# Loads of 48 rows for 40, separate tiles for the first two chunks' products, and later triangular inverses on GpSimd

## The chip, the cores and the metric

The kernel runs on one core of one Trainium2 chip. The metric is the device time of one execution in microseconds. The kernel before takes 633.68 us (median of three runs, 632.99 to 636.66). The core has TensorE (PE, with its weight loads shown as PEld), VectorE (DVE), ScalarE (ACT), GpSimd (POOL) and SyncE (SP). Each engine executes its own list of instructions in order and waits on semaphores for the others. All transfers of this kernel are issued from SP.

## The reference

Inputs are r, k, v, w, a, b with batch 4, heads 8, sequence 768 and head size 40: 32 independent recurrences, each with a state of 40x40. The attention output goes through a layer norm and a two-layer network (320 to 1280 to 320, in the code "moe"), and is added to it.

```python
for t in range(S):
    y[:, :, t] = np.einsum('bhd,bhde->bhe', rt, state)
    Sa = np.einsum('bhde,bhe->bhd', state, at)
    state_decay = state * wt[:, :, None, :] - np.einsum('bhd,bhe->bhde', Sa, bt)
    state = state_decay + np.einsum('bhd,bhe->bhde', vt, kt)
...
xn = (x - mu) / np.sqrt(var + 1e-06) * g_ln
ch = np.maximum(xn @ w_ch1, 0.0) @ w_ch2
return (x + ch)
```

All is fp32. The network's weights and activations are each split into a high and a low part in the reduced format fp32r, and the products are made of these parts.

## The kernel before

The sequence is cut into 24 chunks of 32 steps. The 32 recurrences lie as two halves of 16, each half's 40 head elements on partitions 0 to 39 and 64 to 103 (`ROWS`), so that an instruction over both halves covers partitions 0 to 103. Two chunks make a slab.

For each chunk, `prep(c)` loads `wa` (the decays w and the vectors a) and `bk` (k and b) in two transfers of 40 rows each. VectorE makes the running products of w by two scans with a reciprocal between (L335, L337, L339). `aT` = a times the second scan (L343) and `bk` times the first (L351) are made by VectorE for the first four chunks (`EARLY = 4`) and by GpSimd for the other twenty. `aT` is copied by two DMAs into `abd`, a tile of the other layout, of which there is one; TensorE's product L361 of `bk` and `abd` gives the chunk's two 32x32 triangles for each recurrence, which VectorE masks into `gk` (L364). From `gk` they go by DMA into `d_l` (the triangles to be inverted) and `d_k` in DRAM.

`invert(s)` handles a slab: one DMA brings the slab's `d_l` into `yv`, 64 triangles on 64 partitions. There a memset (L395) and fourteen pairs of small multiply (L403) and add (L407) instructions, with 28 to 112 elements a partition, invert the 16x16 diagonal blocks, each instruction depending on the one before. A copy on ACT (L409) transposes a part, and the result goes through DRAM (`d_h`) into the tiles `hv`. All twelve inversions are on VectorE.

`merge(c)` joins the two diagonal blocks to the inverse of the full triangle on TensorE (L428, L439, with an ACT copy L430 between). `loads(c)` brings the other operands, `x2s` from `aT` and `d_k` among them, and transposes `bk` on TensorE (L464). `chain(c)` is the recurrence from chunk to chunk: products L487, L497, L514 with ACT copies L490 and L501 between, and VectorE's state update L521. `post(c)` gives the chunk's output y (L535, L550, L567, L584, then L588 on VectorE). After each second chunk, `norm` and `moe` follow for the pair: ten groups of eight products L753, an ACT (L756) and a VectorE (L758) step, and six products L737.

`weights()` turns the network's 22 weight pieces, handed over as fp64 words, into fp32 by integer operations on VectorE (L626, L627, L630). For ten pieces it takes the sign by an ACT activation (L621) and a GpSimd product (L634) rather than by the third VectorE operation L630. Then ACT and GpSimd split them (L668, L670, L644, L659).

Every step is recorded as a task with an engine, a key, an estimated length, and what it reads and writes. `Plan.order` then walks through a model of the engines and writes each engine's list: at each step the task that could start first, ties within 0.05 us by the lower key. On PE a rule prefers the network's dense products after a sparse stretch. The chip executes these lists in order; the model's lengths decide the order only. A DMA's place on SP comes from a model of a transfer pipe (`kb` over a rate, and `queue`, how far ahead of it a transfer may be issued). A task named in `after` waits for a mark such as `"first"`, here written by chunk 1's `aT` product, which the loads of chunks 2 and 3 wait for.

Of the kernel before, what the change touches and what calls it, by code (L numbers as in the profile page):

```python
# [11 lines left out]
F32 = mybir.dt.float32  # L12
# [9 lines left out]
C = 32  # L22
# [27 lines left out]
class Plan:  # L50
# [34 lines left out]
    def order(self, free):  # L85
# [31 lines left out]
        while len(out) < len(T):  # L117
# [61 lines left out]
def body(ctx, tc, ea, eb, vr, rd, vt, w1, w1x_in, w2, gl, fe, fd, out):  # L179
# [35 lines left out]
    gk, = ring(1, "gk", 512)  # L215
# [31 lines left out]
    two = lambda x, i, n=2: [(x, i, y) for y in range(n)]  # L247

# [72 lines left out]
    def prep(c):  # L321
        i, s, j, k = c % 2, c // SLAB, c % SLAB, c % BK
        kp = c - 3.4
# [3 lines left out]
        after = [("first",)] if 2 <= c < 4 else []  # L327
        kl = kp + (0.5 if 2 <= c < 4 else -1.0 if c < 2 else 0.0)
        for hf in (1, 0):
            dma(kl - 1.3, 167, after, [W[hf]], t[ROWS[hf]], ea[c, hf])  # L330
        for hf in (1, 0):
            dma(kl - 1.1, 164, after, [K[hf]], tb[ROWS[hf]], eb[c, hf])
        R = slice(0, 104)
        n = 528
        op("DVE", 1.25, kp, W + ["start0"], [("g", i)], lambda: nc.vector.tensor_tensor_scan(  # L335
            out=flat(g[R]), data0=t[R, 0:n], data1=flat(start0[R]), initial=0.0, op0=ALU.mult, op1=ALU.max))
        op("DVE", 0.24, kp, [("g", i)], ["last"], lambda: nc.vector.reciprocal(  # L337
            out=last[R, :, C:33], in_=g[R, :, C:33]))
        op("DVE", 1.25, kp, W + ["last"], [("q", i)] + ([("go",)] if c == 0 else []), lambda: nc.vector.tensor_tensor_scan(  # L339
            out=flat(q[R])[:, ::-1], data0=t[R, n:0:-1], data1=flat(last[R])[:, ::-1], initial=0.0,  # L340
            op0=ALU.mult, op1=ALU.max))
        eng, e, us = ("DVE", nc.vector, 1.0) if c < EARLY else ("POOL", nc.gpsimd, 1.8)
        op(eng, 0.7 * us, kp, W + [("q", i)], A + ([("first",)] if c == 1 else []), lambda: e.tensor_tensor(  # L343
            out=at[R, 0:512].rearrange("p (h t) -> p h t", t=C),
            in0=t[R, 529:1041].rearrange("p (h t) -> p h t", h=16), in1=q[R, :, 1:33], op=ALU.mult))
        for hf, rs in enumerate(ROWS):
            dma(kp + 0.05, 82, A, [("abd", 0, hf)], abd[rs, hf].rearrange("p h t -> p (h t)"), at[rs, 0:512])
        op("ACT", 0.25, kp, [("g", i)], [("pc", c % AT)], lambda: nc.scalar.copy(
            out=at[R, 512:528], in_=g[R, :, C:33].rearrange("p h o -> p (h o)")))
        kb = tb[R].rearrange("p (h x t) -> p h x t", h=16, x=2)  # L350
        op(eng, 1.25 * us, kp, [("g", i)], K, lambda: e.tensor_tensor(  # L351
            out=kb, in0=kb, in1=g[R, :, 0:C].unsqueeze(2).broadcast_to([104, 16, 2, C]), op=ALU.mult))
# [3 lines left out]
        def f(b=b):  # L356
            pg = bank[b.at].rearrange("p (f n t) -> p f n t", f=2, t=C)
            for h in range(8):
                for bb in range(2):
                    p = 8 * bb + h  # L360
                    mm(pg[64 * bb:64 * bb + 64, :, h], lhsT=tb[R, 64 * p:64 * p + 64], rhs=abd[R, :, p],  # L361
                       start=True, stop=True)
        op("PE", 1.08, kp + 0.3, K + two("abd", 0), [b], f, opens=[b], room=["gk"], recs=32)
        op("DVE", 0.68, kp + 0.3, [b, "sign"], ["gk"], lambda b=b: nc.vector.tensor_tensor(  # L364
            out=gk.rearrange("p (n t) -> p n t", t=C), in0=bank[b.at].rearrange("p (n t) -> p n t", t=C),
            in1=sign.unsqueeze(1).broadcast_to([128, 16, C]), op=ALU.mult))
# [13 lines left out]
        op("ACT", 0.62, c - 1.8, [("q", i)], ["qc"], lambda: nc.scalar.copy(  # L380
# [6 lines left out]
    def invert(s):  # L387

        n, c0 = 32 * SLAB, SLAB * s
        k0 = c0 - 2.0  # L390
# [4 lines left out]
        op("DVE", 0.15, k0, (), ["y"], lambda: nc.vector.memset(y[:, 0:1024:33], 1.0))  # L395
        yb = y.rearrange("p (i x) -> p i x", i=2)[:, :, 0:512].rearrange("p i (a t) -> p i a t", t=C)[:, :, :, 0:B]
        for j in range(1, B - 1):
# [3 lines left out]
            def f(j=j, m=m, S=S):  # L401
                tv = tmp[0:n, 0:2 * m * j].rearrange("p (i a t) -> p i a t", i=2, t=j)
                nc.vector.tensor_tensor(  # L403
# [3 lines left out]
                nc.vector.tensor_tensor(out=v, in0=v, in1=tv, op=ALU.add)  # L407
            op("DVE", 0.6, k0 + 0.02 * j, (), ["y", "ytmp"], f)
# [35 lines left out]
    def loads(c):  # L444
        i = c % 2
        at = aT[c % AT]
        for hf, rs in enumerate(ROWS):
            vs = slice(VROW[hf], VROW[hf] + C)
            dma(c - 1.2, 84, [("aT", c % AT), ("pc", c % AT)], [("x2s", i, hf)], x2s[i][rs, hf], at[rs])
# [3 lines left out]
            dma(c - 0.6, 82, (), [("r", i, hf)], x5s[i][rs, hf], rd[c, hf])  # L453
            dma(c - 0.6, 82, (), [("vT", i, hf)], vu[i][rs, :, 0], vr[c, hf])

        tb = bk[c % BK]
        for bb in range(2):
# [8 lines left out]
            op("PE", 0.4, c - 1.2 + 0.1 * bb, two("bk", c % BK) + ["ident"], bs, f, opens=bs, room=X, recs=16)  # L466
# [11 lines left out]
    def chain(c):  # L478
        i, o = c % 2, (c + 1) % 2
        b = Bank("A")  # L480
# [8 lines left out]
        op("PE", 0.75, c, two("x2s", i, 4) + two("S", i, 4) + two("v", i), [b], f, opens=[b], room=[("hn", i)], recs=64)  # L489
        op("ACT", 0.46, c, [b], [("hn", i)], lambda b=b: nc.scalar.mul(  # L490
# [7 lines left out]
        op("PE", 0.72, c, [("tt", i), ("hn", i)], [b], f, opens=[b], room=[("u", i)], recs=64)  # L498
        for q, qs in enumerate(QUADS):
            hf, bb = q % 2, q // 2  # L500
            op("ACT", 0.44, c, [b], [("u", i)], lambda b=b, qs=qs, hf=hf, bb=bb: nc.scalar.copy(  # L501
                out=x2[i][UROW[hf]:UROW[hf] + C, hf, 8 * bb:8 * bb + 8],
                in_=bank[b.at][qs, 0:CH].rearrange("p (h e) -> p h e", e=D)))
        if c + 1 < NCH:
            for bb in range(2):
# [10 lines left out]
                op("PE", 0.75, c, two("xk1", i, 4) + [("eye", i), ("u", i)] + two("S", i, 4) + two("v", i), [b], f, opens=[b],  # L516
# [438 lines left out]
```

## Time and profile before

| | before |
|---|---|
| time, median of 3 runs | 633.68 us |
| profiled execution | 636.37 us |
| its span | 634.6 us |
| mean granted TensorE clock | 0.942 of full speed |
| first triangle product L361 starts | 14.67 us |
| first inversion (L395) starts | 36.93 us |
| first merge L428 starts | 52.07 us |
| busy VectorE / GpSimd | 446.5 / 117.6 us |

All times of the profile count from the start of the span. The profiled execution is 0.4% above the median, and 1.8 us of it lie around the span. A row of a group reads: line, engine, operation, output and inputs with shapes, count; then busy time and mean time of one; then idle time of the engine just before, with what ended most of it. A timeline row has the start and the length ahead and the same idle time in brackets. In the windows, each row is a stretch of the span with its length, each engine's busy time and count of instructions, the granted clock, the DMA engines' share and GB/s.

### The profile page before, as it was taken

What the parts mean: (1) busy time and instruction counts of PE and PEld (TensorE: products, weight loads), DVE (VectorE), ACT (ScalarE), POOL (GpSimd) and SP (SyncE); (2) the same over time, 40 slices, a digit from 0 to 9 for tenths busy, and PEclk for the clock granted to TensorE, in tenths of its full rate; (3) what the DMA queues carried; (4) which work ended last, traced back from release to release, by engine and by line L of the source; (5) the groups of instructions that cost most, each with busy time, mean ns of one, the idle gap of its engine ahead of it and who ended that gap; (6) DMA issues with size and microseconds to landing.
All of it is one profiled execution on the core that took longest, in us unless ns stands there. A gap on an engine that the chain in (4) does not pass through costs nothing.

```text
span 634.6 us, 35137 instructions
## 1 busy us (share of the span) xinstructions
PE 537.4 (85%) x15610; PEld 489.7 (77%) x15610; DVE 446.5 (70%) x1114; ACT 323.6 (51%) x836; POOL 117.6 (19%) x109
## 2 busy tenths in 40 slices
PE   0714875888959989899989999999789899999995
PEld 0514764777858879889989988888779799888995
DVE  7588699996488695595785885864876845967742
ACT  9726756664434454564455355354256545644421
POOL 9108055612021220120221021021022100000000
PEclk9999975798969999999989999799799999999998
DMA  6666667365654554446556356446445445452200
GB/s 170 160 176 171 158 161 206 78 155 121 158 152 125 139 134 106 127 122 156 141 127 163 92 138 151 102 112 159 108 122 143 113 106 119 117 134 79 88 32 25
DMA packets 132205, 81.63 MB, mean 129 GB/s; under 512 B 102736, under 2 KB 108880, under 8 KB 132048
## 3 DMA queue, kind: packets, MB, share of 16 engines
q1 hardware_dynamic: 132048, 79.32, 48.8%
q8 instruction: 124, 2.03, 1.3%
q14 instruction: 33, 0.27, 0.2%
HBM read 51.64 MB, written 12.58 MB: 101 GB/s over the span
## 4 chain that ended last, share of the span: by engine, by line
PE 57%; DVE 16%; issue 8%; SPq 6%; DMA 6%; ACT 4%; POOL 2%; DVEq 0%; ACTq 0%; POOLq 0%
PE bank L737 15%; PE bank L753 13%; SPq L253 6%; PE bank L514 4%; PE bank L567 4%; DVE ytmp L403 3%; DVE yv L407 3%; PE bank L361 3%; PE bank L550 3%; PE bank L584 2%; PE bank L464 2%; PE bank L487 2%; PE bank L439 2%; PE bank L535 2%; PE bank L497 2%
## 5 line engine op out<-in xcount | busy, mean ns | idle before, releaser
L737 PE MATMUL bank<-w,hh 128*128 128x320 f32 x480 | 120.2, 336 | 0.0
L753 PE MATMUL bank<-xh,w 128*128 128x256 f32 x480 | 109.2, 289 | 2.2 <-DVE hl L758 1.7
L756 ACT ACTIVATE hh<-bank 128x256 fp32r<-128x256 f32 x120 | 46.1, 384 | 125.3 <-PE bank L753 123.1
L758 DVE SCALAR_TENSOR_TENSOR hl<-bank,hh 128x256 fp32r<-128x256 f32 x120 | 50.3, 420 | 68.3 <-ACT hh L756 65.6
L753 PEld LDWEIGHTS bank<-xh,w 128*128 128x128 f32 x480 | 83.8, 192 | 3.4 <-DVE hl L758 2.0
L351 POOL TENSOR_TENSOR bk<-bk,gE 104x1024 f32<-104x1024 f32 x20 | 45.9, 2294 | 217.5 <-DMA bk<-in_eb_dram 140.3
L737 PEld LDWEIGHTS bank<-w,hh 128*128 128x128 f32 x480 | 79.7, 196 | 3.8
L737 PE MATMUL bank<-w,hl 128*128 128x320 f32 x240 | 76.1, 317 | 0.1
L753 PE MATMUL bank<-xl,w 128*128 128x256 f32 x240 | 68.4, 285 | 1.2 <-DVE xl L725 1.2
L361 PE MATMUL bank<-abd,bk 104*64 104x64 f32 x768 | 32.1, 245 | 35.8 <-POOL mask L266 14.7
L403 DVE TENSOR_TENSOR ytmp<-yv 64x28 f32<-64x28 f32 (+6 forms) x168 | 43.2, 257 | 23.3 <-issue 11.1
L469 ACT COPY xk<-bank 64x320 f32<-64x320 f32 x96 | 40.2, 418 | 35.3 <-PE bank L464 30.9
L361 PEld LDWEIGHTS bank<-abd,bk 104*64 104x64 f32 x768 | 28.8, 157 | 38.0 <-POOL mask L266 14.6
L521 DVE TENSOR_TENSOR x<-bank,x2s 40x320 f32<-40x320 f32 x92 | 44.6, 485 | 10.6 <-PE bank L514 8.4
L514 PE MATMUL bank<-x,xk 128*40 128x40 f32 (+1 forms) x1472 | 43.1, 220 | 9.2 <-ACT x L501 6.1
L514 PEld LDWEIGHTS bank<-x,xk 128*40 128x40 f32 (+1 forms) x1472 | 36.8, 133 | 15.4 <-ACT x L501 6.8
L553 ACT COPY xk<-bank 40x320 f32<-40x320 f32 x96 | 40.2, 418 | 15.2 <-PE bank L550 13.8
L407 DVE TENSOR_TENSOR yv<-yv,ytmp 64x28 f32<-64x28 f32 (+6 forms) x168 | 43.5, 259 | 5.8
L737 PEld LDWEIGHTS bank<-w,hl 128*128 128x128 f32 x240 | 46.9, 195 | 0.7 <-DVE hl L758 0.6
L753 PEld LDWEIGHTS bank<-xl,w 128*128 128x128 f32 x240 | 46.2, 193 | 1.5 <-DVE xl L725 1.5
L573 DVE TENSOR_TENSOR x5s<-bank,mask 64x256 f32<-64x256 f32 x96 | 40.5, 422 | 9.0 <-PE bank L567 6.7
L335 DVE TENSOR_TENSOR_SCAN gE<-wa,start 104x528 f32<-104x528 f32 x24 | 30.8, 1283 | 20.8 <-DMA wa<-in_ea_dram 11.8
(122 smaller groups left out, 1046.5 us busy)
## 6 DMA issues: line engine op xcount, KB each, us to landing
wa<-in_ea_dram SPq DMA_DIRECT2D x48, 162.7 KB
bk<-in_eb_dram SPq DMA_DIRECT2D x48, 160.0 KB
xk<-xk SPq DMA_DIRECT2D x48, 160.0 KB
x2s<-aT SPq DMA_DIRECT2D x48, 82.5 KB
wa<-in_ea_dram SPq DMA_DIRECT2D x24, 165.0 KB
rbd<-in_rd_dram SPq DMA_DIRECT2D x48, 80.0 KB
x<-in_vt_dram SPq DMA_DIRECT2D x48, 80.0 KB
abd<-aT SPq DMA_DIRECT2D x48, 80.0 KB
```

Source lines behind the costliest of these rows:

```text
L351: op(eng, 1.25 * us, kp, [("g", i)], K, lambda: e.tensor_tensor(out=kb, in0=kb, in1=g[R, :, 0:C].unsqueeze(2).broadcast_to([104, 16, 2, C] ...
L361: mm(pg[64 * bb:64 * bb + 64, :, h], lhsT=tb[R, 64 * p:64 * p + 64], rhs=abd[R, :, p], start=True, stop=True)
L403: nc.vector.tensor_tensor(out=tv, in0=yb[:, :, j + 1:, j:j + 1].broadcast_to(S), in1=yb[:, :, j:j + 1, 0:j].broadcast_to(S), op=ALU.mult)
L407: nc.vector.tensor_tensor(out=v, in0=v, in1=tv, op=ALU.add)
L469: op("ACT", 0.45, c - 1.2 + 0.1 * bb, [bs[hf]], [X[hf]], lambda b=bs[hf], zs=zs, hf=hf, bb=bb: nc.scalar.copy(out=xk[i][zs, 1, hf, 8 * bb: ...
L514: mm(pst[ROWS[hf], h], lhsT=xk[i][FROW[hf], 1, hf, p], rhs=x2[i][FROW[hf], hf, p], start=True, stop=True)
L521: nc.vector.tensor_tensor(out=x2[o][rs, hf, ps], in0=bank[b.at][rs, 0:CH].rearrange("p (h e) -> p h e", e=D), in1=x2s[o][rs, hf, 512 + 8 * ...
L573: op("DVE", 0.4, c + 0.5, [b, "mask"], [("z", i)], lambda b=b, zs=zs, ps=ps, hf=hf, bb=bb: nc.vector.tensor_tensor(out=x5s[i][zs, hf, 8 * ...
L737: mm(bank_of(po[u])[:, 0:CH], lhsT=l[:, us], rhs=ws[f"w2_{f}"][:, x], start=f == 0 and n == 0, stop=f == 9 and n == 2)
L753: mm(ph, lhsT=l, rhs=r, start=n == 0, stop=n == 7)
L756: yield "ACT", 0.39, [phs[f]], [("hh", f % 2)], lambda f=f: nc.scalar.activation(out=hht[f % 2], in_=bank_of(phs[f])[:, 0:256], func=AF.Re ...
L758: yield "DVE", 0.42, [phs[f], ("hh", f % 2)], [("hl", f % 2)], lambda f=f: nc.vector.scalar_tensor_tensor(out=hlt[f % 2], in0=bank_of(phs[ ...
```

## The change

- The loads of `wa` and `bk` and of `x2s` from `aT`, r, `rbd` and v's transposed form, and the copy into `abd`, take 48 rows of each half rather than 40. The host arrays are padded with eight rows; the scans and products cover 112 partitions rather than 104.
- For chunks 0 and 1 VectorE writes a times the second scan into the product's tile itself, in two instructions of 48 rows: chunk 0 into `abd`, chunk 1 into `rbd`. ACT copies it back into `aT`. Chunk 1's `gk` is the otherwise unused third `aT` tile. The mark `"first"` is now written by chunk 1's `gk` and gates chunk 2's loads; a mark `"second"`, at the end of the first inversion, gates chunk 3's.
- `EARLY` is 2: `aT` and `bk` of chunks 2 and 3 are GpSimd's.
- The keys of chunks 0 and 1 in merge, chain, post and norm are lower by 2.0 (`soon`), those of the first inversion by 4.
- Inversions of slabs 1 to 11 are on GpSimd, with the same 29 instructions each.
- All 22 weight pieces take the sign by the third VectorE operation.

```diff
+DP = 48
+LROWS = [slice(r, r + DP) for r in HROW]
-EARLY = 4
+EARLY = 2
...
-                pipe = max(pipe, end + 1.3) + t["kb"] / 200.0
+                pipe = max(pipe, end + 1.3) + t["kb"] / 240.0
...
+    soon = lambda c: 2.0 if c < SLAB else 0.0
...
-        kp = c - 3.4
+        kp = c - 3.4 - soon(c)
-        after = [("first",)] if 2 <= c < 4 else []
+        after = [("first",)] if c == 2 else [("second",)] if c == 3 else []
+        ab, an = (rbd, "rbd") if c == 1 else (abd, "abd")
+        gk, gn = (aT[2][:, 0:512], ("aT", 2)) if c == 1 else (gk1, "gk")
-            dma(kl - 1.3, 167, after, [W[hf]], t[ROWS[hf]], ea[c, hf])
+            dma(kl - 1.3, 200, after, [W[hf]], t[LROWS[hf]], ea[c, hf], queue=low)
...
+        if c < 2:
+            for hf, rs in enumerate(LROWS):
+                op("DVE", 0.7, kp, W + [("q", i)], [(an, 0, hf)], lambda hf=hf, rs=rs: nc.vector.tensor_tensor(
+                    out=ab[rs, hf], in0=t[rs, 529:1041].rearrange("p (h t) -> p h t", h=16), in1=q[rs, :, 1:33],
+                    op=ALU.mult))
+                op("ACT", 0.65, kp + 1.0, [(an, 0, hf)], A, lambda hf=hf, rs=rs: nc.scalar.copy(
+                    out=at[rs, 0:512].rearrange("p (h t) -> p h t", t=C), in_=ab[rs, hf]))
+        else:
...
-        op("DVE", 0.68, kp + 0.3, [b, "sign"], ["gk"], lambda b=b: nc.vector.tensor_tensor(
+        op("DVE", 0.68, kp + 0.3, [b, "sign"], [gn] + ([("first",)] if c == 1 else []), lambda b=b: nc.vector.tensor_tensor(
...
-        k0 = c0 - 2.0
+        eng, e, us = ("DVE", nc.vector, 0.54) if s == 0 else ("POOL", nc.gpsimd, 0.75)
+        k0 = c0 - 2.0 - 2 * soon(c0)
-        op("DVE", 0.15, k0, (), ["y"], lambda: nc.vector.memset(y[:, 0:1024:33], 1.0))
+        op(eng, 0.15, k0, (), ["y"], lambda: e.memset(y[:, 0:1024:33], 1.0))
-            op("DVE", 0.6, k0 + 0.02 * j, (), ["y", "ytmp"], f)
+            op(eng, us, k0 + 0.02 * j, (), ["y", "ytmp"] + ([("second",)] if s == 0 and j == B - 2 else []), f)
...
-                if sel:
-                    nc.scalar.activation(out=hi.bitcast(F32), in_=hi.bitcast(F32), func=AF.Sign)
-                if not sel:
-                    nc.vector.scalar_tensor_tensor(
-                        out=m, in0=hi, scalar=0x80000000, in1=m, op0=ALU.bitwise_and, op1=ALU.bitwise_or)
-            if sel:
-                op("POOL", 0.9, key, [res] + sg, [("ot", mi)], lambda: nc.gpsimd.tensor_tensor(
-                    out=m.bitcast(F32), in0=m.bitcast(F32), in1=hi.bitcast(F32), op=ALU.mult))
...
-    def rows(x):
-        return x.reshape(NCH, 2, 16, C, D).transpose(0, 1, 4, 2, 3)
+    def rows(x, pad=0):
+        y = np.full((NCH, 2, DP, 16, C), pad, np.float32)
+        y[:, :, :D] = x.reshape(NCH, 2, 16, C, D).transpose(0, 1, 4, 2, 3)
+        return y
```

New line numbers that answer to old ones: scans L343, L347 (L335, L339); the products into `abd` and `rbd` L353; `aT` L359 (L343); `bk` L367 (L351); triangle product L379 (L361); `gk` L382 (L364); inversion L415, L423, L427, L429 (L395, L403, L407, L409); merge L448 (L428); `weights` L646, L647, L649 (L626, L627, L630); weight parts L686 (L670).

VectorE's list in the opening, from chunk 1's first scan (before). `gE` and `qE` are the scans' outputs, `bank_144` and `bank_146` the products of chunks 0 and 1:

```order
L335 SCALAR_TENSOR_TENSOR gE_79<-wa_74,start_0_71 104x528
L337 RECIPROCAL last_72<-gE_79 104x16
L339 SCALAR_TENSOR_TENSOR qE_81<-wa_74,last_72 104x528
L343 TENSOR_TENSOR aT_83<-wa_74,qE_81 104x512
L351 TENSOR_TENSOR bk_76<-bk_76,gE_79 104x1024
L364 TENSOR_TENSOR gk_87<-bank_144,sign_70 128x512
L335 SCALAR_TENSOR_TENSOR gE_78<-wa_73,start_0_71 104x528
L364 TENSOR_TENSOR gk_87<-bank_146,sign_70 128x512
```

Between these and the first inversion (L395) stand the rest of chunk 2, chunk 3's scans and products, a weight piece and chunk 2's `gk`. The same place after the change:

```order
L343 SCALAR_TENSOR_TENSOR gE_79<-wa_74,start_0_71 112x528
L345 RECIPROCAL last_72<-gE_79 112x16
L382 TENSOR_TENSOR gk_87<-bank_144,sign_70 128x512
L347 SCALAR_TENSOR_TENSOR qE_81<-wa_74,last_72 112x528
L353 TENSOR_TENSOR rbd_86<-wa_74,qE_81 48x512 x2
L367 TENSOR_TENSOR bk_76<-bk_76,gE_79 112x1024
L382 TENSOR_TENSOR aT_84<-bank_147,sign_70 128x512
L343 SCALAR_TENSOR_TENSOR gE_78<-wa_73,start_0_71 112x528
L345 RECIPROCAL last_72<-gE_78 112x16
L347 SCALAR_TENSOR_TENSOR qE_80<-wa_73,last_72 112x528
L415 MEMSET yv_89 64x32
```

Chunk 0's `gk` moved ahead of chunk 1's second scan, chunk 1's `gk` ahead of chunk 2's scans, and the inversion follows right behind chunk 2's scans.

SP's list from the first `d_l` transfers to the first `yv` load, before (`d_l_176` holds the first slab's triangles; `aT_84` is chunk 2's, `bk_75` chunk 3's, this `wa_73` chunk 4's):

```order
L253 DMA d_l_176<-gk_87 32x16x32 x2
L253 DMA d_k_153<-gk_87 32x512 x2
L253 DMA abd_85<-aT_84 40x512 x2
L253 DMA bk_75<-in_eb_dram 40x1024
L253 DMA wa_73<-in_ea_dram 40x1041
L253 DMA yv_89<-d_l_176 64x1024
```

These are chunk 1's `d_l` and what follows. The same place after (`aT_84` is here chunk 1's `gk`, `wa_73` and `bk_77` are chunk 2's loads):

```order
L257 DMA d_l_176<-aT_84 32x16x32 x2
L257 DMA d_k_153<-aT_84 32x512 x2
L257 DMA wa_73<-in_ea_dram 48x1041 x2
L257 DMA bk_77<-in_eb_dram 48x1024
L257 DMA yv_89<-d_l_176 64x1024
```

The two copies into `abd` and the loads of chunks 3 and 4 are gone from between, and chunk 2's loads have moved there from ahead of `d_l`.

GpSimd's list at the later weight pieces, before (`w_8`, `w_9` are pieces of the second layer, `m` and `ot` their work tiles):

```order
L634 TENSOR_TENSOR m_143<-m_143,r_8_219 128x320
L351 TENSOR_TENSOR bk_75<-bk_75,gE_78 104x1024
L670 TENSOR_TENSOR w_8_1828<-m_143,w_8_1828 128x320
L634 TENSOR_TENSOR ot_141<-ot_141,r_9_220 128x320
L670 TENSOR_TENSOR w_9_1924<-ot_141,w_9_1924 128x320
L343 TENSOR_TENSOR aT_82<-wa_73,qE_80 104x512
L351 TENSOR_TENSOR bk_76<-bk_76,gE_79 104x1024
```

After the change, slab 2's inversion (`yv_89` and `ytmp_90`, a memset and 28 instructions) stands between the last two pieces. Its last three rows and what follows:

```order
L427 TENSOR_TENSOR yv_89<-yv_89,ytmp_90 64x2x2x13
L423 TENSOR_TENSOR ytmp_90<-yv_89 64x28
L427 TENSOR_TENSOR yv_89<-yv_89,ytmp_90 64x2x14
L686 TENSOR_TENSOR w_9_2048<-ot_141,w_9_2048 128x320
L359 TENSOR_TENSOR aT_83<-wa_74,qE_81 112x512
L367 TENSOR_TENSOR bk_76<-bk_76,gE_79 112x1024
```

The signs' products L634 are gone, and piece `w_9` and the `aT` product behind it wait in this list until the 28 instructions of the inversion are through.

More of the change, by code (lines that the diff above doesn't have):

```diff
@@ L488, in f @@
                        rhs=x2[i][RROW[hf], hf, p], start=True, stop=True)
[L489 to L490 removed]
+        op("PE", 0.75, k, two("x2s", i, 4) + two("S", i, 4) + two("v", i), [b], f, opens=[b], room=[("hn", i)], recs=64)
+        op("ACT", 0.46, k, [b], [("hn", i)], lambda b=b: nc.scalar.mul(
             out=hn[i], in_=bank[b.at][:, 0:CH].rearrange("p (h e) -> p h e", e=D), mul=-1.0))
```

137 lines of the change are left out of this document (72 added, 65 removed).

## The prediction

> **What bounds the kernel now.** The page comes first: busy shares, TensorE's row in 40 slices, then the chain that ended last, by engine.
>
> ```profile
> PE 537.4 (85%) x15610; PEld 489.7 (77%) x15610; DVE 446.5 (70%) x1114; ACT 323.6 (51%) x836; POOL 117.6 (19%) x109
> PE   0714875888959989899989999999789899999995
> q1 hardware_dynamic: 132048, 79.32, 48.8%
> PE 57%; DVE 16%; issue 8%; SPq 6%; DMA 6%; ACT 4%; POOL 2%; DVEq 0%; ACTq 0%; POOLq 0%
> ```
>
> TensorE carries most of the chain, but its holes lie in the first third; VectorE's 16% of the chain is mostly there. The windows by stage say how much (columns: length, then busy us of PE, PEld, DVE, ACT, POOL, then granted clock, DMA share, GB/s).
>
> ```profile
> 60.00:123.00 63.00, 43.61 (x1358) 37.71 (x1352) 53.99 (x119) 42.60 (x106) 30.71 (x31) 0.76 0.58 156
> 123.00:184.00 61.00, 49.96 (x1612) 44.66 (x1600) 43.11 (x119) 28.93 (x76) 8.42 (x7) 0.93 0.59 145
> 184.00:548.00 364.00, 344.00 (x10443) 314.74 (x10442) 254.08 (x678) 182.15 (x484) 51.09 (x29) 0.96 0.51 127
> 548.00:634.00 86.00, 78.18 (x1706) 73.73 (x1694) 50.55 (x121) 31.09 (x85) 0.00 (x0) 0.98 0.28 79
> ```
>
> PE is busy in the last four stages for 43.6+50.0+344.0+78.2 = 515.8 us, so for only 21.6 of the first 60. Its work hardly changes, so the gain must come out of its holes: 38 us before 60, 30.4 between 60 and 184, 20.0 up to 548, and 8 in the tail. In 60:123 VectorE is 86% busy: there it is the bound, and PE's granted clock is 0.76.
>
> **Part one: the first two chunks.** The timeline of the opening (start, duration, engine, line; in brackets idle time and its releaser):
>
> ```profile
> 7.76 1.26 DVE L339 TENSOR_TENSOR_SCAN qE<-wa,last 104x528 f32<-104x528 f32 x1
> 9.67 1.22 DVE L351 TENSOR_TENSOR bk<-bk,gE 104x1024 f32<-104x1024 f32 x1
> 10.08 2.22 SPq L253 DMA_DIRECT2D abd<-aT  x2
> 14.67 1.98 PE L361 MATMUL bank<-abd,bk 104*64 104x64 f32 x32 [14.67 <-POOL mask L266]
> 19.56 0.74 SPq L253 DMA_DIRECT2D abd<-aT  x1
> 23.18 1.97 PE L361 MATMUL bank<-abd,bk 104*64 104x64 f32 x32
> 23.48 1.26 DVE L335 TENSOR_TENSOR_SCAN gE<-wa,start 104x528 f32<-104x528 f32 x1 [6.04 <-DMA wa<-in_ea_dram]
> 25.26 0.69 DVE L364 TENSOR_TENSOR gk<-bank,sign 128x512 f32<-128x512 f32 x1 [0.52 <-PE bank L361]
> 26.61 0.86 SPq L253 DMA_DIRECT2D d_l<-gk  x2
> 32.06 0.53 SPq L253 DMA_DIRECT2D yv<-d_l  x1
> 36.93 0.09 DVE L395 MEMSET yv<- 64x32 f32 x1
> 44.42 0.64 ACT L409 COPY yv<-yv 64x256 f32<-64x256 f32 x1 [8.03 <-DVE yv L407]
> 52.07 1.56 PE L428 MATMUL bank<-hv 32*32 32x16 f32 x64 [0.50 <-DMA hv<-d_h]
> L343 DVE TENSOR_TENSOR aT<-wa,qE 104x512 f32<-104x512 f32 x4 | 2.8, 692 | 0.1
> ```
>
> The mask is named beside 14.67, but the product doesn't read it; the copy into `abd`, issued at 10.08, does end about there. Both chunks shared one `abd`, so the second copy (last half issued 19.56) stood behind the first product and d_l, d_k. Without copies, by these durations: scan ends 9.0; the 48-row halves cost what 104 rows cost if time goes by elements per row, 2 x 0.69, to 10.4; `bk` 1.22, to 11.6, when the first product can start (14.67 now, 3 earlier). Chunk 1: first scan and reciprocal to 13.2, chunk 0's gk 13.6 to 14.3, second scan to 15.6, two halves to 17.0, `bk` to 18.2, product to 20.2, gk to 20.9 (25.95 now, 5 earlier). The four copies back to aT go to ACT; its queue holds only constants there.
>
> d_l to yv's issue is 5.45 us now, with four other transfers between; with d_k, wa and one bk between I take 4, so about 25, landing 4.9 later (32.06 to 36.93) at 30. But VectorE has chunk 2's scans ahead of the inversion, and their load now waits for chunk 1's gk: issued near 23, landing near 27, scans to 30. Hence inversion at 30 (36.93 now) and first merge 15.1 later, at 45. **Term one: -7**, bounds -10 (yv alone decides) and -3 (only the first product moves). The copies, d_l and wa queue on SP, so a late gk 1 delays all behind it.
>
> Chunk 3 gets no such lead: its load waits for the end of the first inversion, so the second slab's triangles reach `yv` about when they do now. I give it zero.
>
> **Part two: VectorE relieved, GpSimd loaded.** Groups (busy us, mean ns of one):
>
> ```profile
> L407 DVE TENSOR_TENSOR yv<-yv,ytmp 64x28 f32<-64x28 f32 (+6 forms) x168 | 43.5, 259 | 5.8
> L403 DVE TENSOR_TENSOR ytmp<-yv 64x28 f32<-64x28 f32 (+6 forms) x168 | 43.2, 257 | 23.3 <-issue 11.1 <-DMA d_h<-d_l 3.7 <-DMA x2s<-aT 3.3
> L351 DVE TENSOR_TENSOR bk<-bk,gE 104x1024 f32<-104x1024 f32 x4 | 4.9, 1220 | 0.0
> L630 DVE SCALAR_TENSOR_TENSOR ot<-r,ot 128x256 uint32<-128x256 uint32 x7 | 4.1, 582 | 0.2
> L351 POOL TENSOR_TENSOR bk<-bk,gE 104x1024 f32<-104x1024 f32 x20 | 45.9, 2294 | 217.5 <-DMA bk<-in_eb_dram 140.3 <-DMA hv<-d_h 26.4 <-PE bank L720 20.1
> L343 POOL TENSOR_TENSOR aT<-wa,qE 104x512 f32<-104x512 f32 x20 | 24.6, 1231 | 106.6 <-DVE qE L339 53.5 <-DMA x2s<-aT 15.7 <-DMA x2s<-d_k 14.8
> L659 POOL TENSOR_TENSOR w1x<-ot,w1x 64x320 fp32r<-64x320 f32 x4 | 3.6, 891 | 28.7 <-issue 28.4
> L634 POOL TENSOR_TENSOR ot<-ot,r 128x320 f32<-128x320 f32 x6 | 5.3, 877 | 5.5 <-ACT qm L430 2.8 <-ACT ot L644 1.6 <-ACT w L668 1.1
> L267 POOL TENSOR_SCALAR_AFFINE_SELECT sign<-sign 32x32 f32<-32x32 f32 x4 | 0.8, 207 | 0.3
> ```
>
> VectorE loses 11/12 of 86.7 = 79.5 us, and 2 x (0.69+1.22) = 3.8; it gains 2 x 0.69 for the split products and 10 x 0.58 for the third bit operation of ten weight pieces: net -76, over the whole span. In 60:123 it is 28 x 0.258 = 7.2 less and up to 5.8 more, so VectorE stays loaded there; what goes is that the weight conversions stand behind an 11 us block. In 123:184 two blocks go, 14 us of 43. ACT sheds ten Sign activations, GpSimd ten products of 0.88.
>
> GpSimd's price for the small triangle operations isn't in the trace. Through 512 and 1024 elements a line has 2.08 ns an element and 168 ns fixed; 28 operations average 80 elements (sum of 2j(15-j) over 14 steps = 1120), so 0.33 us, and with 0.07 us of hand-over about 11.3 us an inversion: an estimate. Below: the select's 207 ns for 32 elements gives 28 x 0.28 = 7.8. Above: L659's 891 ns for 320 elements gives 27. I take the line, since both its points are two-operand products in fp32 on this engine; the upper end stays in the range.
>
> What an inversion may last is read at a steady one:
>
> ```profile
> 338.20 0.69 DVE L364 TENSOR_TENSOR gk<-bank,sign 128x512 f32<-128x512 f32 x1
> 348.86 0.09 DVE L395 MEMSET yv<- 64x32 f32 x1
> 360.43 0.67 ACT L409 COPY yv<-yv 64x256 f32<-64x256 f32 x1 [0.76 <-DVE yv L407]
> 370.43 0.72 PE L428 MATMUL bank<-hv 32*32 32x16 f32 x64
> ACT yv L409 <- DVE yv L407: 20.9, 7, 8.0
> PE bank L514 <- ACT x L501: 6.1, 3, 4.8
> ```
>
> It lasts 11.6 us on VectorE, since other work is mixed in, and 32.2 from gk to merge. GpSimd at 11.3, plus at most one chunk's `aT` and `bk` (3.5) ahead of it, is 11 to 15. I put the break-even at 16, an estimate: 11.6 and some 4 us of the waits that come back between landing and merge. Beyond it ACT's copy L409 waits, with the state's copies queued behind it, and TensorE behind those (the last row's 6.1 us).
>
> **Term two, 60 to 184: -10**, a third of the 30.4 us of holes; bounds 0 (GpSimd returns it) and -20. **Term three, 184 to 548: -6**, under a third of the 20.0; bounds -18 and, for slow inversions, the rival's price.
>
> A port conflict shows in the trace:
>
> ```profile
> 116.25 2.29 POOL L351 TENSOR_TENSOR bk<-bk,gE 104x1024 f32<-104x1024 f32 x1
> 116.51 2.37 DVE L627 SCALAR_TENSOR_TENSOR ot<-r,ot 128x320 uint32<-128x320 uint32 x1
> ```
>
> The VectorE operation ends when GpSimd's does plus its own length. With 28 short operations an inversion, VectorE waits for 0.33 us at a time rather than 2.3, but GpSimd waits a whole scan of 1.26. Two chunks' scans inside an inversion add up to 5 us to its 11.3: 16, the break-even. The Trainium skill, "SBUF — State Buffer", section "SBUF: two separate sides", says that VectorE operations with two SBUF inputs and GpSimd hold the shared port pair exclusively for a whole instruction. These two rows agree; it speaks against this change.
>
> **Part three: loads of 48 rows.** At most all bytes of the queue grow by a fifth: 48.8% becomes 58.6%, what 60:184 bears already. I take zero, bounds -3 and +3. The row for a gain:
>
> ```profile
> DVE gE L335 <- DMA wa<-in_ea_dram: 11.8, 5, 6.0
> ```
>
> The Trainium skill, "DMA: Bandwidth & Descriptors", section "Why a DMA increments its semaphore by 16 and not by 1", says that a transfer uses the largest number of engines up to 16 that divides its slowest dimension: 10 for 40 rows, 16 for 48, so 4 rows each become 3. By it the sum would be about 3 us lower (a quarter of 11.8); no row here counts engines.
>
> **The sum.** -7-10-6 = -23 from the profiled execution's 636.37 (span 634.6 and 1.8 around it): 613.4. The median, 633.68, is 0.42% below that execution, so 611.
>
> **Rivals.** (a) *GpSimd's inversions are late.* At 0.70 us an operation (nearer to L659's 0.89), an inversion is 19.6, 3.6 over the break-even; ten slabs make +36, less terms one and two, 17: 636.4+19 = 655, so 653. It decides from 16 us upward, and overtakes the gains at 16+1.7. For: the upper row, the locked port. Against: the line. The Trainium skill, "GPSIMD Engine Reference", section "Performance pitfalls for Q7 kernels", charges 50% more an element when reads step over 8 bytes, as these do; by it 13.7 us, still under 16.
> (b) *Only the opening moves.* TensorE is 94.5% busy in 184:548, and conversions and GpSimd's weight parts refill the middle: -7, so 627.
> (c) *TensorE closes its holes.* With the middle at -20 and the stage to 548 at -18: -45, so 589. For: VectorE's 76 us; against: the chain of state remains.
> (d) *Exchange without gain.* The early weight conversions, now all on VectorE, and weight parts standing behind an inversion on GpSimd eat term one: 632 to 636.
>
> **Chances.** Forecast 0.48, (a) 0.09, (b) 0.20, (c) 0.13, (d) 0.10. A change under 1% (627.3 to 640.0) can hardly be told from none. Forecast and (c) are faster, (b) straddles the bound and is put at 0.12 faster, 0.08 same; (d) is same. Faster 0.73, same 0.18, slower 0.09. The forecast's own range is 600 to 623; the range 590 to 634 takes in (b), most of (c) and (d), and leaves out (a).
>
> **What would show it.** First products at about 11.6 and 18, first merge near 45; inversion from memset to ACT's copy 11 to 15 us on GpSimd, mean operation 0.33; VectorE busy near 370; PE's holes in 60 to 184 cut by a third; PE's busy time unchanged within 1%. The forecast is wrong if the mean operation is over 0.5 us, if ACT's wait for the inversions grows beyond the 20.9 us of before, or if the holes of 60 to 184 stay near 30 us.

## The result and the profile after

The changed kernel takes 685.25 us (median of four, 681.11 to 690.38) against 634.66 us in the same comparison: 1.08 times the time before, 95% interval 1.071 to 1.089. The forecast was 611, range 590 to 634. It missed the sign. Rival (a) had the sign and 653. Here and below a time is the median of all executions of a run, while a ratio with its interval leaves out executions in a slower state that some fall into and compares with the kernel before in the same comparison, so the two need not agree to the last figure.

The page after the change, the rows that answer to those of before:

```profile
span 681.8 us, 35117 instructions
PE 555.0 (81%) x15610; PEld 506.3 (74%) x15610; DVE 374.9 (55%) x803; ACT 318.6 (47%) x830; POOL 229.6 (34%) x422
PE   1514793789689979959989989899799898799996
q1 hardware_dynamic: 142640, 86.88, 54.7%
PE 36%; POOL 14%; DMA 13%; SPq 13%; DVE 9%; issue 8%; ACT 6%; POOLq 0%; DVEq 0%; ACTq 0%
```

VectorE was relieved as forecast, to 374.9 us, and the kernel is slower all the same. TensorE's share of the chain fell from 57% to 36%. GpSimd (2% before) has 14%, transfers and their issue on SP have 26% (12% before). The span grew by 47.2 us: 17.6 are more busy time of PE with the same instructions (mean granted clock 0.912 for 0.942), 29.6 are more holes. By stage (columns as before):

```profile
60.00:123.00 63.00, 42.01 (x1346) 37.30 (x1346) 51.39 (x96) 38.89 (x100) 34.27 (x53) 0.74 0.70 170
123.00:184.00 61.00, 51.82 (x1579) 46.69 (x1574) 38.10 (x74) 27.34 (x73) 31.86 (x64) 0.87 0.74 152
184.00:548.00 364.00, 323.91 (x9520) 295.49 (x9521) 177.62 (x408) 166.49 (x446) 125.00 (x236) 0.92 0.56 131
548.00:681.00 133.00, 117.93 (x2648) 110.17 (x2646) 66.64 (x159) 49.47 (x131) 11.19 (x29) 0.95 0.32 85
```

The holes up to 184 are what they were within 2 us (70.9 for 68.8). Between 184 and 548, the stage where I had seen 6 us to gain, they doubled from 20.0 to 40.1. The steady inversion answering to the one shown of before, from the slab's second gk to its merge (timeline; the last row is the DMA into `hv`):

```profile
452.33 0.69 DVE L382 TENSOR_TENSOR gk<-bank,sign 128x512 f32<-128x512 f32 x1
466.97 0.15 POOL L415 MEMSET yv<- 64x32 f32 x1
480.26 0.63 ACT L429 COPY yv<-yv 64x256 f32<-64x256 f32 x1 [4.02 <-POOL yv L427]
482.40 0.41 ACT L523 COPY x<-bank 32x320 f32<-32x320 f32 x1
490.44 0.20 PE L448 MATMUL bank<-hv 32*32 32x16 f32 x2 [1.75 <-DMA hv<-d_h]
486.94 1.84 SPq L257 DMA_DIRECT2D hv<-d_h  x4
```

38.1 us from gk to merge for 32.2. The inversion lasts 13.3 us for 11.6, from the memset to ACT's copy. ACT stands idle for 4.0 of them with the state's copies L523 queued behind it. One slab isn't the rule: of the 5.9 us more, 4.0 lie ahead of its inversion. On the mean of the fourth to the eleventh slab, gk to memset takes 13.1 us for 12.3, and memset to last add 12.6 for 10.5. What else waits is in the view of waits (total, times, longest):

```profile
DVE gE L343 <- DMA wa<-in_ea_dram: 47.2, 10, 10.2
ACT yv L429 <- POOL yv L427: 34.5, 10, 4.8
PE bank L448 <- DMA hv<-d_h: 19.5, 10, 10.5
```

Before, VectorE waited 11.8 us for `wa`, and ACT 20.9 us for the inversions. So two candidates stand side by side: inversions that end late for ACT, and transfers that land late for VectorE and TensorE.

### The profile page after: what moved, and what is told of

It reads as the page before. It is cut to its first block, busy times and chain, and to the rows that moved or that the text cites. A ratio compares the mean times of both kernels' runs of the same rounds, so it can differ in the third digit from the quotient of the medians.

```text
span 681.8 us, 35117 instructions
## 1 busy us (share of the span) xinstructions
PE 555.0 (81%) x15610; PEld 506.3 (74%) x15610; DVE 374.9 (55%) x803; ACT 318.6 (47%) x830; POOL 229.6 (34%) x422
## 4 chain that ended last, share of the span: by engine, by line
PE 36%; POOL 14%; DMA 13%; SPq 13%; DVE 9%; issue 8%; ACT 6%; POOLq 0%; DVEq 0%; ACTq 0%
SPq L257 12%; PE bank L769 10%; PE bank L753 9%; POOL ytmp L423 6%; POOL yv L427 6%; DMA yv<-d_l 4%; PE bank L590 2%; PE bank L536 2%; DMA wa<-in_ea_dram 2%; DMA hv<-d_h 2%; PE bank L379 2%; DMA abd<-aT 1%; PE bank L607 1%; PE bank L573 1%; PE bank L448 1%
## 5 line engine op out<-in xcount | busy, mean ns | idle before, releaser
L753 PE MATMUL bank<-w,hh 128*128 128x320 f32 x480 | 123.4, 344 | 0.0
L769 PE MATMUL bank<-xh,w 128*128 128x256 f32 x480 | 114.9, 300 | 0.6 <-ACT xh L740 0.6
L367 POOL TENSOR_TENSOR bk<-bk,gE 112x1024 f32<-112x1024 f32 x22 | 51.0, 2319 | 165.1 <-DMA bk<-in_eb_dram 106.8
L769 PEld LDWEIGHTS bank<-xh,w 128*128 128x128 f32 x480 | 89.4, 205 | 1.7 <-ACT xh L740 1.0
L343 DVE TENSOR_TENSOR_SCAN gE<-wa,start 112x528 f32<-112x528 f32 x24 | 33.4, 1396 | 61.8 <-DMA wa<-in_ea_dram 47.2
L423 POOL TENSOR_TENSOR ytmp<-yv 64x28 f32<-64x28 f32 (+6 forms) x154 | 60.1, 391 | 11.2
L427 POOL TENSOR_TENSOR yv<-yv,ytmp 64x28 f32<-64x28 f32 (+6 forms) x154 | 55.6, 361 | 12.1
L490 ACT COPY xk<-bank 64x320 f32<-64x320 f32 x96 | 40.1, 418 | 34.9 <-PE bank L485 33.4
L543 DVE TENSOR_TENSOR x<-bank,x2s 40x320 f32<-40x320 f32 x92 | 44.6, 485 | 13.8 <-PE bank L536 11.6
L359 POOL TENSOR_TENSOR aT<-wa,qE 112x512 f32<-112x512 f32 x22 | 26.1, 1186 | 76.1 <-DMA x2s<-aT 41.6
L769 PEld LDWEIGHTS bank<-xl,w 128*128 128x128 f32 x240 | 49.5, 206 | 0.3 <-DVE xl L741 0.3
L379 PE MATMUL bank<-abd,bk 104*64 104x64 f32 x736 | 31.4, 247 | 20.9 <-DMA x<-in_vt_dram 12.2
L576 ACT COPY xk<-bank 40x320 f32<-40x320 f32 x96 | 40.1, 417 | 15.4 <-PE bank L573 13.9
L523 ACT COPY x<-bank 32x320 f32<-32x320 f32 x96 | 40.0, 416 | 12.9 <-PE bank L519 11.4
```

The source lines that it names most:

```text
L423: e.tensor_tensor(out=tv, in0=yb[:, :, j + 1:, j:j + 1].broadcast_to(S), in1=yb[:, :, j:j + 1, 0:j].broadcast_to(S), op=ALU.mult)
L427: e.tensor_tensor(out=v, in0=v, in1=tv, op=ALU.add)
L543: nc.vector.tensor_tensor(out=x2[o][rs, hf, ps], in0=bank[b.at][rs, 0:CH].rearrange("p (h e) -> p h e", e=D), in1=x2s[o][rs, hf, 512 + 8 * ...
L753: mm(bank_of(po[u])[:, 0:CH], lhsT=l[:, us], rhs=ws[f"w2_{f}"][:, x], start=f == 0 and n == 0, stop=f == 9 and n == 2)
L769: mm(ph, lhsT=l, rhs=r, start=n == 0, stop=n == 7)
```

## The experiments

**The inversions back on VectorE (e1), the inversions alone on GpSimd (e2).**

```diff
 e1, changed kernel:
-        eng, e, us = ("DVE", nc.vector, 0.54) if s == 0 else ("POOL", nc.gpsimd, 0.75)
+        eng, e, us = ("DVE", nc.vector, 0.54)
 e2, kernel before:
+        eng, e, us = ("DVE", nc.vector, 0.6) if s == 0 else ("POOL", nc.gpsimd, 0.75)
...
-                nc.vector.tensor_tensor(out=v, in0=v, in1=tv, op=ALU.add)
+                e.tensor_tensor(out=v, in0=v, in1=tv, op=ALU.add)
```

> The changed kernel with all twelve inversions on VectorE, nothing else undone. Theory one (GpSimd's inversions, 12.8 us from memset to last add, hold up the merges and with them the state): 625 to 640, at least 45 of the 51 us come back. Theory two (the transfers: more bytes in the loads of 48 rows and another order on SP hold up scans and merges): 665 to 685, since all transfers stay.

> The kernel before with only the inversions of slabs 1 to 11 moved to GpSimd. Theory one: 665 to 695, the whole loss with none of the other edits. Theory two: 630 to 645.

e1: 669.72 us, 1.057 [1.049, 1.065]. e2: 654.69 us, 1.029 [1.021, 1.038]. e1 lies in theory two's range, e2 between the two. Neither theory holds alone: of some 50 us, GpSimd's inversions explain 15 to 20.

**40 rows in the changed kernel (e3), and a shorter inversion in unchanged lists (e4).**

```diff
 e3:
-DP = 48
+DP = 40
-        LR = slice(0, 112)
+        LR = slice(0, 104)
 e4:
+            skip = s > 0 and j % 2 == 1 and j < B - 2
...
+                if skip:
+                    return
```

> The changed kernel with loads, scans and products of 40 and 104 rows as before; GpSimd keeps its inversions. Theory one: 675 to 690, no change. Theory two: 635 to 655.

> The changed kernel with six of the fourteen pairs left out in the inversions of slabs 1 to 11 (those of steps 1, 3, 5, 7, 9 and 11; this part of the inverse is not computed). Every engine's list is otherwise the same, row by row, so this run has no other order. An inversion lasts about 7.3 us in place of 12.8. Theory one: 11 slabs get 5.5 us each sooner, 630 to 655. Theory two, or a loss that comes from the order alone: 675 to 690.

e3: 678.68 us, 1.070 [1.062, 1.077]. e4: 666.04 us, 1.051 [1.041, 1.061]. With six of the fourteen pairs gone and every list as it was, an inversion lasts 6.6 us on average for 12.7. 11 slabs x 6.1 us gave back only 19 us, though no wait of ACT for GpSimd's inversions is left. So the length of the inversion does set part of the pace, a little under a third of a microsecond per microsecond, and something else sets the rest.

**The other parts, each alone: the gate of chunk 3 (e5), the opening (e6), 48 rows (e7), the conversions (e8).** The three on the kernel before take over the change's own lines for that part (in e8 these also enter VectorE's three operations on a piece as three tasks rather than one); of each, the line that marks it:

```diff
 e5, changed kernel:
-        after = [("first",)] if c == 2 else [("second",)] if c == 3 else []
+        after = [("first",)] if 2 <= c < 4 else []
 e6, kernel before (with the lines for chunks 0 and 1 that follow from it, and soon):
+EARLY = 2
+        after = [("first",)] if c == 2 else [("second",)] if c == 3 else []
 e7, kernel before:
+            dma(kl - 1.3, 200, after, [W[hf]], t[LROWS[hf]], ea[c, hf])
 e8, kernel before:
-                    nc.scalar.activation(out=hi.bitcast(F32), in_=hi.bitcast(F32), func=AF.Sign)
```

> The changed kernel, with chunk 3's loads again waiting only for chunk 1's triangles (mark first), not for the end of the first inversion (mark second). In the changed kernel chunk 3's gk ends at 73.7 us, before at 52.4. Theory three (this gate delays the second slab by some 20 us, and the delay is never made up): gk of chunk 3 near 52 to 56, total 650 to 668. If the delay is absorbed later, 675 to 690.

> The kernel before with the opening edits alone: two chunks' products written into their tiles, EARLY 2, the lower keys, chunk 2 waiting for first and chunk 3 for second; 40 rows, the old conversions, all inversions on VectorE, the old transfer rate. Theory three: 645 to 660, most of the 35 us that stayed with the inversions back on VectorE. My first forecast for this part was 627; if the loss lies in the rows, the conversions or the transfer rate, 622 to 636.

> The kernel before with the padded arrays and loads, scans and products of 48 and 112 rows, nothing else. By the trace of the change (scans 1.40 for 1.28 to 1.47 us, 86.9 for 79.3 MB): 636 to 645; if transfers carry the rest of the loss, 655 or more; by the rule that 48 rows use more engines, 625 to 632.

> The kernel before with the sign of all 22 weight pieces taken by VectorE's third operation, nothing else. VectorE gets 5.8 us more in its fullest stretch, ACT and GpSimd lose 5 and 10: 632 to 642. If the early VectorE load carries the rest of the loss, 650 or more.

e5: 678.27 us, 1.060 [1.049, 1.071]. e6: 643.95 us, 1.011 [1.005, 1.016]. e7: 648.54 us, 1.018 [1.010, 1.027]. e8: 630.55 us, 0.987 [0.979, 0.995].

The opening loses where I had taken 7 us. In e6, chunk 3's gk and chunk 2's output, then the same two before the change (VectorE's timeline):

```profile
73.67 0.69 DVE L382 TENSOR_TENSOR gk<-bank,sign 128x512 f32<-128x512 f32 x1
145.49 0.49 DVE L611 TENSOR_TENSOR xt<-bank,pi 128x320 f32<-128x320 f32 x1
```

```profile
51.66 0.69 DVE L364 TENSOR_TENSOR gk<-bank,sign 128x512 f32<-128x512 f32 x1 [0.67 <-DMA hv<-d_h]
123.75 0.49 DVE L588 TENSOR_TENSOR xt<-bank,pi 128x320 f32<-128x320 f32 x1 [0.67 <-PE bank L584]
```

The second slab comes 22 us late; later chunks make up most of it, and 1.1% remain. Undoing the gate alone in the changed kernel (e5) gave back 7 us by the medians and 2% by the ratios (1.060 for 1.080, intervals that just touch), less than theory three asked for. Chunk 3's gk moved only from 73.00 to 63.59 there, where theory three had 52 to 56. The 48 rows lose without any other edit; the page of e7:

```profile
q1 hardware_dynamic: 142896, 87.27, 59.4%
PE 54%; DVE 13%; DMA 12%; issue 7%; SPq 6%; ACT 5%; POOL 0%; DVEq 0%; ACTq 0%; POOLq 0%
```

10% more bytes take 24% more of the engines' time (59.4% of 645.5 us for 48.8% of 634.6), and transfers' share of the chain doubles from 6% to 12%. Only the conversions gain, and little is to spare: their interval ends at 0.995.

**The transfer assumption of the ordering (e9, e10), the gainful parts of the opening (e11), and GpSimd's price in the ordering (e12).**

```diff
 e9, changed kernel:
-                pipe = max(pipe, end + 1.3) + t["kb"] / 240.0
+                pipe = max(pipe, end + 1.3) + t["kb"] / 200.0
 e10, kernel before: 200.0 to 240.0 on the same line
 e11, from e6, with the conversions of e8:
-EARLY = 2
+EARLY = 4
+    soon = lambda c: 0.0
+        after = [("first",)] if 2 <= c < 4 else []
 e12, from e2:
-        eng, e, us = ("DVE", nc.vector, 0.6) if s == 0 else ("POOL", nc.gpsimd, 0.75)
+        eng, e, us = ("DVE", nc.vector, 0.6) if s == 0 else ("POOL", nc.gpsimd, 0.95)
```

> The changed kernel with the old assumption on transfers in the ordering (200 for 240 KB a us, so the order of all engines changes, the work doesn't). The four parts tried alone on the kernel before come to +20, +7, +12 and -8 us, +31 together, where the whole change costs 50. If the assumption carries the rest: 655 to 670. If the rest is that the parts make each other worse (an inversion on GpSimd behind later transfers): 675 to 690.

> The kernel before with the new assumption (240 for 200), nothing else. If it carries the rest: 645 to 655. If the parts make each other worse: 628 to 640.

> The kernel before with the gainful parts alone: the first two chunks' products written into their own tiles without DMA, and all signs on VectorE; 40 rows, EARLY 4, the old keys, both loads waiting for first, inversions on VectorE. If the opening's loss came from chunks 2 and 3 being held back: first merge near 45 to 48, gk of chunk 3 near 46 to 52, total 618 to 630. If direct products bring nothing to the end: 628 to 634, as with the conversions alone.

> The kernel before with the inversions of slabs 1 to 11 on GpSimd as in e2, but the ordering reckons with 0.95 us a pair, near the 0.91 measured, in place of 0.75. If e2's loss comes from lists that expect the inverse too early (ACT's copy and TensorE's merge standing in front of other work): 630 to 642. If the latency itself, or VectorE and GpSimd waiting for each other, costs it: 648 to 660.

e9: 673.02 us, 1.053 [1.046, 1.059]. e10: 641.54 us, 1.004 [1.000, 1.009]. e11: 631.64 us, 0.989 [0.983, 0.996], no better than the conversions alone. e12: 634.06 us, 0.989 [0.984, 0.995]: the same work on the same engines as e2, and e2's 20 us are gone. ACT's waits, first e2, then e12:

```profile
ACT yv L410 <- POOL yv L408: 26.3, 9, 6.8
```

```profile
ACT yv L410 <- POOL yv L408: 3.1, 1, 3.1
```

The number is only an entry in the ordering. At 0.75 a pair the lists reckon with an inversion of 10.65 us; e2's lasted 12.6 on average where its copy waited. With 0.95 the lists put more network work ahead of ACT's copy: the last slab's copy stands behind 95 of the 120 network groups in e12, and behind 86 in e2. In the kernel before, GpSimd isn't too slow; the lists expected it too early.

**Does the price explain the changed kernel (e13, e14), and does it act without GpSimd (e16)?** e14 has e3's edit, the 200 of e9 and the 0.95; e15 is e11 with e12's line.

```diff
 e13, changed kernel:
-        eng, e, us = ("DVE", nc.vector, 0.54) if s == 0 else ("POOL", nc.gpsimd, 0.75)
+        eng, e, us = ("DVE", nc.vector, 0.54) if s == 0 else ("POOL", nc.gpsimd, 0.95)
 e16, kernel before:
-            op("DVE", 0.6, k0 + 0.02 * j, (), ["y", "ytmp"], f)
+            op("DVE", 0.42, k0 + 0.02 * j, (), ["y", "ytmp"], f)
```

> The changed kernel with 0.95 for 0.75 us a pair in the ordering, nothing else; all work the same. Theory four (the lists reckon with an inversion of 10.5 us where the chip takes 12.5 to 12.8, and ACT's copy, standing too early, stops its queue): ACT's wait for GpSimd's inversions falls from 34.5 to under 10 us and the total to 650 to 665; the 48 rows and the opening stay. If the price mattered in e12 by chance: 675 to 690.

> The changed kernel with 0.95, with 40 rows, and with the old transfer assumption of 200; opening edits, conversions and GpSimd's inversions stay. Theory four with the single parts (opening +7, conversions -8, inversions -3): 625 to 642. If the parts make each other worse, 655 or more.

> A candidate: the products into their own tiles and all signs on VectorE as in e11, and the inversions of slabs 1 to 11 on GpSimd priced at 0.95; 40 rows, EARLY 4, old keys and gates. Theory four: 622 to 632, under the kernel before and near or under e11. If GpSimd's latency costs by itself: 640 or more.

> A control without GpSimd: the kernel before, with 0.42 for 0.60 us a pair in the ordering, inversions on VectorE. Theory four in general form (a price 20 to 30% under the chip's costs some per cent): 645 to 660, ACT's wait for the inversions above 30 us. If only GpSimd's place matters: 630 to 642.

e13: 678.00 us, 1.062 [1.054, 1.069]. e14: 640.26 us, 1.006 [1.002, 1.011]. e15: 645.21 us, 1.013 [1.009, 1.018]. e16: 655.07 us, 1.029 [1.022, 1.036].

e16 is the control: no GpSimd, no other work, only a price lowered by 30%, and the loss is e2's. ACT's wait there:

```profile
ACT yv L409 <- DVE yv L407: 36.0, 12, 8.1
```

The kernel before reckons short too, with 8.55 us for the fourteen pairs and the memset, where they take 10.1 on average, other work of VectorE's list included; its ACT waits 20.9 us. In e16 it is 6.03 for 9.9.

e13 failed as I had put it, and lies in the range that I had given for chance. The wait I blamed is gone, but the two waits for transfers stand, and nearly so does the time (waits of e13, then of e14):

```profile
DVE gE L343 <- DMA wa<-in_ea_dram: 36.8, 11, 10.1
PE bank L448 <- DMA hv<-d_h: 22.8, 9, 10.2
ACT yv L429 <- POOL yv L427: 2.2, 1, 2.2
```

```profile
DVE gE L343 <- DMA wa<-in_ea_dram: 24.9, 7, 6.1
PE bank L448 <- DMA hv<-d_h: 13.1, 4, 10.2
ACT yv L429 <- POOL yv L427: 3.5, 1, 3.5
```

e15 shows that single gains of 1% don't add: the conversions (e8), the conversions with the direct products (e11) and the priced GpSimd inversions (e12) were 1.3%, 1.1% and 1.1% under the kernel before, and all together are 1.3% over it. I have no cause for that beyond the new order of all lists. Every new entry rewrites that order, and the order alone moves the time: the transfer rate, which changes no work, by 5 us in e10 and by 12 in e9. The higher price was the faster one each time, by 21 us in e12, 18 in e16 and 7 in e13, but the last is no more than the rate can do.

**Price or transfer assumption, and whether a lower rate mends the 48 rows (e17, e18).** e17 is e3 with 0.95; e18 is e13 with 160 for 240.

> The changed kernel with 40 rows and 0.95 us a pair, the transfer assumption still 240: it stands between e3 (40 rows, 0.75, 240: 679) and e14 (40 rows, 0.95, 200: 640). If the price of the inversion makes the gap: 636 to 648. If the transfer assumption makes it: 668 to 680. Each half: near 660.

> The changed kernel with its 48 rows, 0.95 us a pair, and transfers reckoned at 160 KB a us in place of 240 (e13 has 240 and 678). If the 48 rows cost through lists that expect the data too early: VectorE's wait for wa falls under 25 us from 36.8, total 640 to 660. If the larger transfers cost by themselves: 665 to 685.

e17: 648.98 us, 1.021 [1.009, 1.032]. e18: 672.20 us, 1.059 [1.049, 1.068]. The changed kernel's rows and price now make a square, at 240 throughout (medians in us, ratios in brackets):

| | 0.75 a pair | 0.95 a pair |
|---|---|---|
| 48 rows | 685 (1.080) | 678 (e13, 1.062) |
| 40 rows | 679 (e3, 1.070) | 649 (e17, 1.021) |

Each alone gives back 7 us, both together 36, and 200 for 240 another 9 (e14). With all three undone the kernel is 0.6% above the one before. In e18 VectorE's wait for `wa` is short:

```profile
DVE gE L343 <- DMA wa<-in_ea_dram: 10.3, 3, 7.1
```

The wait fell under the 25 us I had named and the time stayed, so data expected too early doesn't explain the cost of the 48 rows by itself. Nor do the waits measure the loss at all. e17 has those of e13 and is 29 us faster, and e12, at 634 us, has a long one for `wa` (two rows of e17, then one of e12):

```profile
DVE gE L343 <- DMA wa<-in_ea_dram: 37.9, 11, 10.8
PE bank L448 <- DMA hv<-d_h: 19.6, 8, 9.9
```

```profile
DVE gE L335 <- DMA wa<-in_ea_dram: 31.6, 10, 6.4
```

The scans aren't longer for the eight rows either: the two take 1.48 and 1.48 us on average in e13, 1.44 and 1.63 in e17. What makes the 48 rows dear is open: it wasn't tried at other row counts, nor with single loads widened.

## Why the prediction was wrong

Of the three signs that the prediction named for being wrong, two came: ACT's wait for the inversions grew to 34.5 us, and the holes of 60 to 184 stayed at 30.2. The third, a mean operation over 0.5 us, did not (0.38). A term was missing as well: TensorE's busy time was to stay within 1% and grew by 3.3%, 17.6 of the span's 47.2 us, with a lower granted clock. No run separates that part.

**Part one, term one (-7).** The first products came as worked out (12.17 and 18.91 for 11.6 and 18.2), the rest did not. Opening of the changed kernel:

```profile
12.17 1.97 PE L379 MATMUL bank<-abd,bk 104*64 104x64 f32 x32 [12.17 <-DMA x<-in_vt_dram]
18.91 1.97 PE L379 MATMUL bank<-rbd,bk 104*64 104x64 f32 x32 [4.11 <-ACT aT L356]
20.92 0.69 DVE L382 TENSOR_TENSOR aT<-bank,sign 128x512 f32<-128x512 f32 x1 [2.11 <-PE bank L379]
23.69 1.47 SPq L257 DMA_DIRECT2D d_l<-aT  x2
26.22 0.91 SPq L257 DMA_DIRECT2D wa<-in_ea_dram  x2
31.78 1.26 DVE L343 TENSOR_TENSOR_SCAN gE<-wa,start 112x528 f32<-112x528 f32 x1 [10.17 <-DMA wa<-in_ea_dram]
34.66 0.09 DVE L415 MEMSET yv<- 64x32 f32 x1
45.42 0.69 DVE L382 TENSOR_TENSOR gk<-bank,sign 128x512 f32<-128x512 f32 x1 [0.44 <-issue]
51.53 1.67 PE L448 MATMUL bank<-hv 32*32 32x16 f32 x64 [10.49 <-DMA hv<-d_h]
73.00 0.69 DVE L382 TENSOR_TENSOR gk<-bank,sign 128x512 f32<-128x512 f32 x1
```

I had named the right bound, VectorE's scans of chunk 2 ahead of the inversion, and put its load too early: issued near 23 and landed near 27, against 26.22 and scans at 31.78. So the inversion came 2.3 us earlier, not 7, and the merge 0.5 us (51.53 for 52.07). And I gave chunk 3 zero. Chunk 2's gk now stands behind the whole inversion (45.42 for 35.14), and chunk 3's came 21 us later (73.00 for 51.66). This part alone costs 1.1% (e6).

**Part two, GpSimd's price.** The estimate was good: a price line through the two large products gave 0.226 and 0.401 us for 28 and 112 elements. Undisturbed rows of one inversion:

```profile
371.39 0.24 POOL L423 TENSOR_TENSOR ytmp<-yv 64x28 f32<-64x28 f32 x1
376.25 0.40 POOL L423 TENSOR_TENSOR ytmp<-yv 64x112 f32<-64x112 f32 x1
```

That inversion takes 11.6 us (371.32 to 382.93), and the slowest 13.7, inside my 11 to 15. The 0.07 us of hand-over, which no row stood for, is about what lies between two of its operations (0.07 to 0.09). The Trainium skill, "GPSIMD Engine Reference", section "Performance pitfalls for Q7 kernels", adds 50% an element for reads that step over 8 bytes, and its remedy speaks of the innermost step. The prediction was wrong to put these reads under it: by the kernel's access patterns their innermost step is 0 or 4 bytes in all pairs but the first, and the row of 112 elements shows no such addition. The conflict shows in the means (0.391 and 0.361 us for 0.33):

```profile
467.37 1.09 POOL L427 TENSOR_TENSOR yv<-yv,ytmp 64x28 f32<-64x28 f32 x1
468.53 1.10 POOL L423 TENSOR_TENSOR ytmp<-yv 64x52 f32<-64x52 f32 x1
```

```profile
467.07 1.33 DVE L343 TENSOR_TENSOR_SCAN gE<-wa,start 112x528 f32<-112x528 f32 x1 [0.81 <-POOL bk L367]
468.33 1.24 DVE L347 TENSOR_TENSOR_SCAN qE<-wa,last 112x528 f32<-112x528 f32 x1
```

Two operations of 0.23 and 0.28 us take 1.1 beside two scans, and each ends 0.06 us after its scan. That agrees in direction with the rule on the shared port pair that the prediction quotes from the Trainium skill, "SBUF — State Buffer", section "SBUF: two separate sides"; an operation that only began behind its scan would end 0.23 or 0.28 us after it.

**The break-even of 16 us** is the step that failed here. I compared the inversion's length with what it had on VectorE, and took spare time between landing and merge as margin. What decides in the kernel before is the length that the lists reckon with. They were written for 10.65 us; an inversion that ends later stops ACT's queue, with the state's copies behind it. e12 and e16 show that this price alone moves the time by some 3% either way, with GpSimd and without. In the changed kernel it moved 30 us with 40 rows (e17 for e3) and 7 with 48 (e13). So inversions of 12.6 us cost 20 us in e2, where I had allowed up to 16 for nothing.

**Term three (-6)** went with it and with part three: the stage to 548 lost 20 us of PE's time. **Term two (-10)**: the holes of 60 to 184 stayed at 30 us. VectorE's relief is real and didn't shorten them; the conversions, which I had booked as VectorE's burden, were the one part that gained (e8, 1.3%), by a mechanism that I didn't follow.

**Part three (zero, bounds -3 and +3)** was mis-sized: +1.8% alone (e7), and 29 us of the changed kernel once the price is right (e13 against e17). The queue's rows of e13 and e17:

```profile
q1 hardware_dynamic: 142640, 86.88, 55.4%
q1 hardware_dynamic: 131848, 79.00, 47.6%
```

10% more bytes took 22% more of the engines' time (55.4% of 678.9 us, 47.6% of 648.3). I had bounded bytes and time alike by a fifth, a share of 58.6%, and e7 came to 59.4%. So the bound was near, and the step that failed is the one from there to zero: I took a mean share that another stage bears for no cost, and it cost 11 us alone (e7). The gain of 3 us that the rule on engines in the Trainium skill, "DMA: Bandwidth & Descriptors", section "Why a DMA increments its semaphore by 16 and not by 1", would give is not in these runs, and no row of them counts engines.

**The sum** treated the parts as additive. They aren't: alone on the kernel before, the ratios of e2, e6, e7, e8 and, for the transfer rate, e10 come to +4.9%, and together to 8.0%; rows and price hide each other in the square above.

**Rival (a)** had the right place and a wrong condition. It asked for 0.70 us an operation; the chip had 0.38 and was late all the same. (b) to (d) fell.

## What to carry to other kernels

When a program's order is written by a model, moving work to another engine changes two things, the work and the model's entry for it; read the entry against the chip's own time for the whole chain of dependent steps, waits included (here 0.75 against 0.91 us a pair), before blaming the engine. Too early a place in an in-order list can cost as much as more work: look for the wait of the small copy (ACT's 34.5 us) and for what is queued behind it. But let a run, not the wait, say what it is worth: e13 lost 32 us of this wait and gained 7. When a loss has several sources, removing one may show little (685 to 678) until the other is gone too (to 649), so test them in pairs.

The fastest median seen in this study is the kernel before with the conversions alone (e8, 630.55 us, 0.987 [0.979, 0.995]).

## What the runs showed of the hardware beyond that

Padding loads from 40 to 48 rows raised the transfer engines' busy time by more than twice the share of the bytes: from 309 to 376 us of all sixteen for 79.0 to 86.9 MB (e17 and e13), 37 to 42 ns a packet and engine; e7 has 383 us for the 310 of the kernel before. GpSimd's two-operand fp32 products followed one line from 28 to 1024 elements a partition, 0.17 us and 2.1 ns an element (0.24, 0.40, 1.23 and 2.29 us for 28, 112, 512 and 1024).
